# A linear-attention block and a gated GLU on one core: VectorE's work on the turned denominators, the weight forms and b's seeds is offered later, and small loads change queues

## The chip, the cores and the metric

The kernel runs on one core of one Trainium2 chip. A core has five engines with a queue of instructions each: TensorE (matrix products, into PSUM), VectorE, ScalarE, GpSimd and SyncE (SP). In the profile they are PE, DVE, ACT, POOL and SP. DMA transfers are issued from SP's and from GpSimd's queue here. Engines wait for each other by semaphores; an engine that waits holds everything behind in its own queue. The metric is the time of one execution in microseconds; lower is better.

## The reference

With S = 2048 tokens of width D = 640, 32 heads of width 20, and F = 1536, the output is `g * a + (1 - g) * b`, where `g` is one gate per token:

```python
g = _sigmoid((x * gate_w).sum(-1, keepdims=True))
phi = lambda t: jnp.where(t > 0, t + 1, jnp.exp(t)) + 1e-6
# a: linear attention
kv = jnp.einsum("bhsd,bhse->bhde", phi(k), v)
z = jnp.einsum("bhsd->bhd", phi(k))
num = jnp.einsum("bhqd,bhde->bhqe", phi(q), kv)
den = jnp.einsum("bhqd,bhd->bhq", phi(q), z)[..., None] + 1e-6
a = (num / den).transpose(...).reshape(B, S, D) @ wo
# b: gated linear unit
h = _sigmoid(x @ w_gate) * (x @ w_up)
b = h @ w_down
```

Each token and head has one denominator `den`, a sum over the 20 features of phi(q) weighted by `z`. All is float32.

## The kernel before

**Numbers and products.** Every float32 operand of a product is split into a high and a low part in TensorE's faster float32 format, and a product is three matmuls (`mm3`: high by high, high by low, low by high; lines 417 to 419). The high part is made by ScalarE (line 433), the low part by a subtraction on VectorE (line 437). On top of this, the products use Strassen- and Winograd-like schemes of seven products in place of eight, so there are many sums of operands on VectorE and of results in PSUM. A `Block` has seven such products, its steps `s1` to `s7`, of six or nine matmuls each.

**Stages.** Tokens come in four groups of 512 (g = 0 to 3). First the keys and the matrix phi(k)^T x are made (to about 140 us of the trace). Then, for the token groups 2 and 3 (`pr` = 1) and after that for 0 and 1 (`pr` = 0), the queries are made (`q_phase`), and then b's GLU in `f_phase`: twelve chunks f of 128 hidden columns, with steps (f, 1) to (f, 7). Odd chunks also carry the products with `w_down` of the pair before (`down_pair`, four parts d0 to d3). In the second `f_phase`, chunks 1 to 11 are `EBlock`s, which fold the fifth part of the inner dimension into fewer matmuls (line 428) with the help of weight forms ("e" forms): three small VectorE operations of 128 x 128 on pieces `d` and `u` of the weights that are loaded from DRAM (`queue_e`, line 1435 and on). Step s3 is the first that reads them. Last comes the attention product: phi(q), divided by the denominator and multiplied by the gate, is multiplied by the matrix M made of kv and wo (`ABlock`, `a_unit`). It accumulates in PSUM on a start value, "b's seed", which is b times the gate row 1 - g (`seed_b`).

**Denominators.** `queue_dens` is called in the second `f_phase`, in chunk 2 for groups 2 and 3 and in chunk 7 for groups 0 and 1. It sums phi(q), loaded as `pden` from DRAM, with weights `zcol` into `fac` (five operations a group), stores the sum (`den_dram`), loads it back turned, in four parts of 32 partitions (`turn_in`, `fac<-den_dram`), adds the four column blocks, takes the reciprocal, multiplies by the gate rows `gs` (`factor`, line 1609 and on), stores that (`fac_dram`) and loads it back four times over (`turn_out`, `fac<-fac_dram`). `pq_scale` multiplies phi(q) by `fac` later (line 441, `pl<-pl,fac` and `hf<-hf,fac`).

**The order of the work.** Nothing is ordered at run time: each engine runs its queue in program order. A planner in Python (`Order`) makes that order while the program is built. It keeps a clock for TensorE, ScalarE and VectorE with fixed costs (`v_cost(w)` is 0.07 us and w / 960), and between TensorE's steps, in `fill`, it puts the VectorE and ScalarE items in that it has been given. An item has a cost, a function, a key and a function `ready`: it is not placed before TensorE's or its own engine's clock has reached that time, and not when its engine would end more than a slack (0.6 us on ScalarE, 1.2 us on VectorE) behind TensorE. There are several lists: urgent items (`first`), streams with a due time, the plain list, then a lazy list, a `chain` (only its first item may be placed; the denominators are here) and a spare list (forms of M, through the single buffer `mt`). A stream's item is placed without regard to the slack 2 us ahead of its due time. `need(key)` places an item at once, where TensorE's next step needs it.

The planner believes times for DMAs too (`Rings`, `Ring`, from line 316): two rings, SP's with 0.38 us per issue and a lag of 1.5 us, GpSimd's with 0.55 us and 2.2 us, shared bandwidth, and 0.5 us at the end. `order.when(x)` is the time at which x is believed to have landed:

```python
took = 1.25 * max(1, n // r) * (7 + 0.0377 * r) / 16e3
self.cell = self.rings.issue(self.n, start + self.lag, took)
```

Here n is a transfer's bytes and r the bytes of a run. For some items a margin is added to that time already: `DEN_LAG = 5.0` (line 315) for the five sums of a denominator, for the stores out of `mt`, half of it for M's rows. If a transfer lands later than believed, the instruction that reads it stands on its engine and waits, with everything behind it.

**Loads at the end of the second `f_phase`.** After its last step the code issues, on SP, `load_p(3)`, `load_m(1)` (960 KB of M's forms into `ws`), `load_b(2)` (three loads of 256 KB, `bl<-b_dram`), the gate row of group 3, `load_b(3)` and `load_ms(0)`; the gate rows of groups 0 and 1 (`omg<-gate_dram`) are loaded later, after the first half of the attention blocks of groups 2 and 3.

Of the kernel before, what the change touches and what calls it, by code (L numbers as in the profile page):

```python
# [14 lines left out]
P = 128  # L15
S, D, F = 2048, 640, 1536
H, DH = 32, 20
KC = D // P
# [296 lines left out]
DEN_LAG = 5.0  # L315
# [65 lines left out]
def v_cost(w):  # L381
    return 0.07 + w / 960

@with_exitstack
def gated_mix_kernel(ctx: ExitStack, tc: tile.TileContext, x0, xt, xn, wk, wv, wo, wst_q, wst_f, out_t):
# [6 lines left out]
    order = Order()  # L392
    rings = Rings()
    sp, gp = Ring(nc.sync, order, rings, 0, 0.38, 1.5), Ring(nc.gpsimd, order, rings, 1, 0.55, 2.2)

    def f32(ap):
        return ap.bitcast(F32)
# [37 lines left out]
    def vec2(out, a, b, op, after=""):  # L435
        order.on_vec(width(out), after, 1.0, out, a, b)
        nc.vector.tensor_tensor(out, a, b, op=op)  # L437

    def vec3(out, a, scalar, b, op0, op1, after=""):
        order.on_vec(width(out), after, 1.0, out, a, b)  # L440
        nc.vector.scalar_tensor_tensor(out, a, scalar, b, op0=op0, op1=op1)

    def vec1(out, a, s0, s1=None, op0=OP.mult, op1=None, after=""):
        order.on_vec(width(out), after, 1.0, out, a)
        if op1 is None:
            nc.vector.tensor_scalar(out, a, s0, None, op0=op0)
        else:
            nc.vector.tensor_scalar(out, a, s0, s1, op0=op0, op1=op1)
# [10 lines left out]
    def add(out, a, b, after=""):  # L459
        vec2(out, a, b, OP.add, after)  # L460
# [11 lines left out]
    def fac_tile(dt=F32):  # L472
        return common.tile([P, NG, TG], dt, name="fac", tag="fac")

    fac = fac_tile()
# [6 lines left out]
    gate_rep = dram.tile([S // P, H, P], F32, name="gate_rep")  # L482
    den_dram = dram.tile([P, NG, TG], F32, name="den_dram")
    fac_dram = dram.tile([P, NG, P], F32, name="fac_dram")
# [588 lines left out]
    g = GTBatch(0, [0])  # L1073
# [8 lines left out]
    for c in range(1, 4):  # L1082
        ck = chunks[c]
        if c == 1:
# [14 lines left out]
            g = GTBatch(c, batches[c])  # L1099
# [59 lines left out]
        if c == 3:  # L1159
# [15 lines left out]
            W, WT = {}, {}  # L1175
# [22 lines left out]
        if c > 1:  # L1198
            g = GTBatch(c, batches[c])
# [53 lines left out]
    def tt(name, dt=F32, shape=(P, TG)):  # L1253
        return pw.tile(list(shape), dt, name=name, tag="t", bufs=4)

    def ct(name, dt=F32, shape=(P, TG)):
        return pw.tile(list(shape), dt, name=name, tag="c", bufs=5)
# [177 lines left out]
    def queue_e(f):  # L1435

        n = ("f", 0, f)
        d, u = EW[f, "d"], EW[f, "u"]
        dh, dl = d[:, :P], d[:, P:]
        uh, ul = (W[n, 1][c][:, 2 * P:] for c in range(2))  # L1440

        def fn():
            vec3(u[:, :P], f32(dh), -1 / UP, f32(ul), OP.mult, OP.add)
            vec3(u[:, P:], f32(ul), UP, f32(uh), OP.mult, OP.add)
            vec3(dl, f32(dh), 1 / UP, f32(dl), OP.mult, OP.add)
        order.add(0, 3 * v_cost(P), fn, ("e", f), lambda: max(order.when(d), order.when(WT[n, 1])),
                  stream=("e", f), due=order.due((0, f, 3)))

    def queue_et(late):
# [125 lines left out]
    def queue_dens(*gs2):  # L1575

        nonlocal fac
        if "f" in EF:
            EF.pop("f")
            fac = fac_tile()  # L1580
        st = {}

        def load(g, u):
            if u < KC:
                st[g, u] = tt("pden")
                gp.dma_start(st[g, u], p_dram[:, u, g])
                st["at", g, u] = lambda: order.when(st[g, u])

        def one(g, u):
            td = fac[:, g]  # L1590
            if u == 0:
                vec1(td, st[g, u], zcol[:, 0:1], zeps[:, 0:1], OP.mult, OP.add)
            else:
                vec3(td, st[g, u], zcol[:, u:u + 1], td, OP.mult, OP.add)
            load(g, u + 2)
            if u == KC - 1:
                gp.dma_start(den_dram[:, g], td)
                st["at", g, u + 1] = lambda: order.when(den_dram[:, g])

        def turn_in(g):  # L1600
            for j in range(4):
                js = slice(j * H, (j + 1) * H)
                gp.dma_start(fac[js, g].rearrange("h (d c) -> h d c", c=P),
                                  den_dram[:, g, j * P:(j + 1) * P].rearrange("(d h) c -> h d c", h=H))
            st[g, "gs"] = tt("gs")[:, :P]
            sp.dma_start(st[g, "gs"], gate_rep[4 * g:4 * g + 4].rearrange("i h c -> (i h) c"))
            st["at", g, KC + 1] = lambda: max(order.when(fac[:, g]), order.when(st[g, "gs"]))

        def factor(g):
            td = fac[:, g]  # L1610
            q = td[:, :P]
            add(td[:, :2 * P], td[:, :2 * P], td[:, 2 * P:])
            add(q, q, td[:, P:2 * P])
            order.on_vec(5 * P, "")
            nc.vector.reciprocal(q, q)
            vec2(q, q, st[g, "gs"], OP.mult)
            gp.dma_start(fac_dram[:, g], q)
            st["at", g, KC + 2] = lambda: order.when(fac_dram[:, g])

        def turn_out(g):  # L1620
            for d in range(4):
                sp.dma_start(fac[d * H:(d + 1) * H, g].rearrange("h (j c) -> h j c", c=P),
                                  fac_dram[:, g].rearrange("(j h) c -> h j c", h=H))
        order.add(0, 0, lambda: [load(g, u) for u in range(2) for g in gs2], chain=True)
        for u in range(KC):
            for g in gs2:
                order.add(0, v_cost(TG), lambda g=g, u=u: one(g, u), None, lambda g=g, u=u: st["at", g, u]() + DEN_LAG, chain=True)
        for n, (v, fn) in enumerate(((0, turn_in), (2.0, factor), (0, turn_out))):
            for g in gs2:
                order.add(0, v, lambda g=g, fn=fn: fn(g), ("fac", g) if n == 2 else None,  # L1630
                          lambda g=g, n=n: st["at", g, KC + n](), chain=True)

    sp.t = max(sp.t, gp.cell[0])
    load_w()
# [457 lines left out]
    OMG = {}  # L2092
# [17 lines left out]
    def load_omg(g):  # L2110

        OMG[g] = down_pool[1].tile([P, TG], F32, name="omg", tag="omg") if g == 2 else tt("omg")
        sp.dma_start(OMG[g], gate_dram[1, g * TG:(g + 1) * TG].partition_broadcast(P))
# [281 lines left out]
    def f_phase(pr, q, hooks={}):  # L2395
# [86 lines left out]
        for f in range(FC):  # L2482
# [3 lines left out]
            if f in dens[pr]:  # L2486
                queue_dens(*dens[pr][f])
# [88 lines left out]
    q = q_phase(1, lambda k: [(b12h[:, k], b12l[:, k])], extra)  # L2576
# [32 lines left out]
    q = q_phase(0, lambda k: [tuple(t[:, k] for t in b12)], {0: [lambda: next(down), more_c], 1: [lambda: next(down)], 8: [lambda: order.need((nx[1], 6), False), early_omg], 9: [lambda: queue_ds(LAST), lambda: queue_df(LAST)], 10: [lambda: queue_last("T2", "T3", "T4")]})  # L2609

    groups = (2, 3, 0, 1)
    PL, PQ, BL, MHL, PT, MS, X3, ST = {}, {}, {}, {}, {}, {}, [], []

    def x2_tile(name="pl", dt=F32):
        return px.tile([P, 2, TG], dt, name=name, tag="x2", bufs=10)
# [4 lines left out]
    def load_m(i):  # L2620

        while any(it[3] == "m" for it in order.spare) or order.pend:
            order.need("m")
            order._flush()
        n = (0, 7, 10)
        t = (wf_tile, ws_tile)[i]().rearrange("p a b -> p (a b)")[:, :(n[i + 1] - n[i]) * D]
        for j0, j1 in ((0, 4), (4, 7), (7, 10))[2 * i:2 + i]:
            sp.dma_start(f32(t[:, (j0 - n[i]) * D:(j1 - n[i]) * D]),
                         mp_dram.rearrange("p a b c -> p (a b c)")[:, j0 * D:j1 * D])
        for j in range(n[i], n[i + 1]):  # L2630
            MHL[divmod(j, 2)] = t[:, (j - n[i]) * D:(j - n[i] + 1) * D]
# [40 lines left out]
    def load_b(g):  # L2672

        if g < 2:
            BL[g] = {o: tb[:, o, g] for o in range(KC)}
        else:
            if g == 2:
                t = x2_tile("bl")
                BL[g] = {4: ct("bl"), 0: t[:, 0], 2: t[:, 1]}
            else:  # L2680
                t = down_pool[1].tile([P, D], F32, name="mr", tag="mr")
                BL[g] = {4: t[:, :TG]}
            for o, t in BL[g].items():
                sp.dma_start(t, b_dram[:, o, g - 2])
# [19 lines left out]
    def pq_tiles(g):  # L2704

        t = [x2_tile("pq", F32R) for _ in range({2: 4, 3: 2}.get(g, KC))]
        PQ[g] = [(x[:, 0], x[:, 1]) for x in t]
        if g == 2:
            X3.extend(x3_tile("pq") for _ in range(4))
            PQ[g].append((X3[2][:, 2], X3[3][:, 2]))  # L2710
        elif g == 3:
            PQ[g] += [(X3[0][:, u], X3[1][:, u]) for u in range(3)]
# [56 lines left out]
        vec2(ps, BL[g][o], OMG[g], OP.mult)  # L2769

    def b_at(g, o):
        return max(order.when(BL[g][o]), order.when(OMG[g]) if g in OMG else 1e9)

    def queue_seed(g, o, tag):
        order.add(0, v_cost(TG), lambda: seed_b(g, o, tag), ("b", g, o), lambda: b_at(g, o), first=True)
# [153 lines left out]
    pq_tiles(2)  # L2929
    queue_pq(2)  # L2930
    load_p(3)
    load_m(1)
    pq_tiles(3)
    queue_scale(3)
    queue_pq(3)
    load_b(2)
    load_omg(3)
    load_b(3)
    load_b(0)
# [105 lines left out]
```

## Time and profile before

| | |
|---|---|
| three runs | 730.4, 733.19, 735.96 us; median 733.19 |
| profiled execution | 734.18 us; the span from its first to its last instruction 732.5 us |
| TensorE clock granted in it | 0.998 of full |
| TensorE busy | 721.5 us, 98% of the span |
| VectorE busy | 589.2 us, 80% |
| ScalarE busy | 366.1 us, 50% |
| GpSimd busy (its DMA issues among it) | 118.0 us, 16% |
| DMA | 177.6 MB, 242 GB/s on the mean |

The second `f_phase` lies between about 445 and 640 us of the trace, the attention product between 659 and 729. In the profile's views a line such as `DVE fac L437 <- DMA fac<-den_dram: 6.4, 1, 6.4` says who waited (engine, the tile it writes, the line of the kernel), for whom, and how long in total, how often, and the longest. In a timeline the first number is the start in microseconds from the span's start, the second the duration; what stands in brackets is the engine's idle time just before and what ended it. `out<-in` are the kernel's own names of the tiles. Matmuls overlap, so the step from start to start is shorter than one matmul's duration. Most operations are recorded at the line of a helper (417 to 419, 428: matmuls; 433: ScalarE; 437, 441, 448: VectorE; 374: DMA issues).

### The profile page before, as it was taken

The page shows a single profiled execution, that of the slowest core. Times are in us where ns is not written, and L with a number is a line of the kernel's source. Part 1 is how long each engine was busy: PE and PEld are TensorE (multiplying, and loading weights), DVE is VectorE, ACT ScalarE, POOL GpSimd, SP SyncE. Part 2 cuts the span into 40 slices and gives each one's busy share as a digit, 9 for nine tenths or more (in the row PEclk, how much of TensorE's full clock was granted, in tenths as well). Part 3 has the DMA queues.
Part 4 walks back from the last instruction along what each step waited for, and adds up shares of the span by engine and source line. Part 5 has one row for each costly group of instructions (what it writes and reads, how often), then busy time and mean ns, then how long its engine had stood idle before and what let it go on. Part 6 is the DMA issues. An engine that isn't in the chain of part 4 may idle for free.

```text
span 732.5 us, 9922 instructions
## 1 busy us (share of the span) xinstructions
PE 721.5 (98%) x3401; PEld 607.3 (83%) x3401; DVE 589.2 (80%) x1045; ACT 366.1 (50%) x682; POOL 118.0 (16%) x199
## 2 busy tenths in 40 slices
PE   9999999999999999999999999998999999999898
PEld 8999999888888888888888888886788888887676
DVE  4988878987777889888998886665776888689886
ACT  5764749267557644444456762363332333335351
POOL 0311111113212211211121122013001131000200
PEclk9999999999999999999999999999999999999999
DMA  8474658698787856657688787889588897779623
GB/s 269 116 205 112 177 137 259 158 326 297 278 323 258 308 205 230 244 221 263 246 330 277 218 287 271 325 283 316 190 250 296 284 323 247 256 287 330 124 42 130
DMA packets 75657, 177.60 MB, mean 242 GB/s; under 512 B 12266, under 2 KB 34170, under 8 KB 73430
## 3 DMA queue, kind: packets, MB, share of 16 engines
q1 hardware_dynamic: 55654, 104.03, 43.5%
q0 software_dynamic: 19664, 72.70, 29.0%
q8 instruction: 27, 0.44, 0.2%
q10 hardware_dynamic: 288, 0.23, 0.1%
q14 instruction: 24, 0.20, 0.1%
HBM read 104.62 MB, written 67.33 MB: 235 GB/s over the span
## 4 chain that ended last, share of the span: by engine, by line
PE 92%; DVE 3%; DMA 2%; ACT 1%; issue 1%; POOL 0%; SPq 0%; DVEq 0%; POOLq 0%; ACTq 0%
PE ch L418 10%; PE ch L419 10%; PE ch L417 10%; PE cc L418 7%; PE cc L419 7%; PE cc L417 7%; PE dd L417 7%; PE dd L418 7%; PE dd L419 7%; PE rot L419 5%; PE rot L418 5%; PE rot L417 5%; PE ch L428 1%; PE cc L428 1%; DMA fac<-den_dram 1%; DMA omg<-gate_dram 1%
## 5 line engine op out<-in xcount | busy, mean ns | idle before, releaser
L437 DVE TENSOR_TENSOR hf<-c,hf 128x512 fp32r<-128x512 f32 x77 | 52.6, 687 | 26.0 <-ACT hf L433 25.5
L433 ACT ACTIVATE hf<-c 128x512 fp32r<-128x512 f32 (+1 forms) x79 | 48.8, 625 | 39.6 <-DVE c L437 39.6
L433 ACT ACTIVATE c<-ch 128x512 f32<-128x512 f32 x43 | 25.7, 597 | 77.8 <-PE ch L428 56.9
L417 PE MATMUL ch<-xth,ws 128*128 128x512 f32 x108 | 42.2, 391 | 0.0
L419 PE MATMUL ch<-xth,ws 128*128 128x512 f32 x108 | 42.1, 390 | 0.0
L418 PE MATMUL ch<-xtl,ws 128*128 128x512 f32 x108 | 42.1, 389 | 0.0
L437 DVE TENSOR_TENSOR tb<-rot,tb 128x512 f32<-128x512 f32 x60 | 39.0, 684 | 1.9 <-PE rot L419 1.9
L437 DVE TENSOR_TENSOR c<-cc,c 128x512 f32<-128x512 f32 x38 | 26.2, 688 | 17.0 <-ACT c L433 10.1
L437 DVE TENSOR_TENSOR c<-c,c 128x512 f32<-128x512 f32 x48 | 33.0, 688 | 2.6 <-ACT c L433 2.0
L437 DVE TENSOR_TENSOR tb<-dd,tb 128x512 f32<-128x512 f32 x41 | 28.1, 686 | 8.3 <-PE dd L419 8.3
L433 ACT ACTIVATE dd<-ch 128x512 f32<-128x512 f32 x22 | 12.8, 583 | 36.2 <-PE ch L428 20.4
L433 ACT ACTIVATE c<-dd 128x512 f32<-128x512 f32 x21 | 12.5, 597 | 35.6 <-PE dd L428 17.0
L417 PE MATMUL dd<-xrh,wg 128*128 128x512 f32 x73 | 28.7, 394 | 1.5 <-ACT dd L433 1.5
L437 DVE TENSOR_TENSOR wst<-wst 128x256 f32<-128x256 f32 (+2 forms) x69 | 27.4, 412 | 1.4
L418 PE MATMUL dd<-xrl,wg 128*128 128x512 f32 x73 | 28.4, 390 | 0.0
L419 PE MATMUL dd<-xrh,wg 128*128 128x512 f32 x73 | 28.4, 389 | 0.0
L417 PE MATMUL cc<-xbh,ws 128*128 128x512 f32 x71 | 27.6, 389 | 0.0
L418 PE MATMUL cc<-xbl,ws 128*128 128x512 f32 x71 | 27.6, 389 | 0.0
L419 PE MATMUL cc<-xbh,ws 128*128 128x512 f32 x71 | 27.6, 389 | 0.0
L433 ACT ACTIVATE c<-c 128x512 f32<-128x512 f32 x31 | 19.5, 628 | 10.5 <-DVE c L437 10.2
L433 ACT ACTIVATE cx<-ch 128x512 f32<-128x512 f32 x16 | 9.6, 597 | 29.1 <-PE ch L419 28.9
L419 PEld LDWEIGHTS ch<-xth,ws 128*128 128x128 f32 x108 | 20.3, 188 | 4.5 <-DVE ws L437 0.3
(755 smaller groups left out, 2403.2 us busy)
## 6 DMA issues: line engine op xcount, KB each, us to landing
wf<-ws POOLq DMA_DIRECT2D x12, 1152.0 KB, 7.7
wst<-wst_f SPq DMA_DIRECT2D x12, 640.0 KB, 4.9
wf<-wg POOLq DMA_DIRECT2D x12, 640.0 KB, 6.8
wd<-wd POOLq DMA_DIRECT2D x12, 640.0 KB, 8.1
wg<-wf SPq DMA_DIRECT2D x12, 640.0 KB, 6.2
wf<-wd SPq DMA_DIRECT2D x10, 640.0 KB, 7.8
ws<-wf SPq DMA_DIRECT2D x23, 256.0 KB, 4.8
xnst<-xn SPq DMA_DIRECT2D x16, 320.0 KB, 4.1
```

The source lines that it names most:

```text
L417: nc.tensor.matmul(out, l_hi, r_hi, start=first, stop=False, skip_group_check=True)
L418: nc.tensor.matmul(out, l_hi, r_lo, start=False, stop=False, skip_group_check=True)
L419: nc.tensor.matmul(out, l_lo, r_hi, start=False, stop=last, skip_group_check=True)
L428: nc.tensor.matmul(out, w, x, start=False, stop=n == len(singles) - 1, skip_group_check=True)
L433: nc.scalar.activation(out, src, fn, **kw)
L437: nc.vector.tensor_tensor(out, a, b, op=op)
```

## The change

Five things are edited; no computation is added or left out.

- The "e" weight forms become ready 5 us (`DEN_LAG`) after their pieces are believed to have landed.
- The gate rows `gs` are loaded from GpSimd's queue instead of SP's, and so are the four parts of `turn_out`.
- `factor` becomes two items of the chain: the two adds (`factor`), and the reciprocal, the multiplication by `gs` and the store (`turn_over`). Their stated costs are 0.6 and 0.9 in place of 2.0. The adds become ready 5 us after the parts of `turn_in` (and `gs`) are believed to have landed; `turn_over` is ready at any time, but as the chain goes in order, it comes after both groups' adds.
- b's seeds (and the scaling of b by the gate row) become ready 2.5 us after the gate row is believed to have landed, or with b, whichever is later.
- `load_m(1)` is issued after `load_b(2)` instead of before `pq_tiles(3)`.

```diff
-        order.add(0, 3 * v_cost(P), fn, ("e", f), lambda: max(order.when(d), order.when(WT[n, 1])),
+        order.add(0, 3 * v_cost(P), fn, ("e", f), lambda: max(order.when(d), order.when(WT[n, 1])) + DEN_LAG,
                   stream=("e", f), due=order.due((0, f, 3)))
...
             st[g, "gs"] = tt("gs")[:, :P]
-            sp.dma_start(st[g, "gs"], gate_rep[4 * g:4 * g + 4].rearrange("i h c -> (i h) c"))
+            gp.dma_start(st[g, "gs"], gate_rep[4 * g:4 * g + 4].rearrange("i h c -> (i h) c"))
             st["at", g, KC + 1] = lambda: max(order.when(fac[:, g]), order.when(st[g, "gs"]))
 
         def factor(g):
...
             add(td[:, :2 * P], td[:, :2 * P], td[:, 2 * P:])
             add(q, q, td[:, P:2 * P])
+
+        def turn_over(g):
+            q = fac[:, g, :P]
             order.on_vec(5 * P, "")
             nc.vector.reciprocal(q, q)
             vec2(q, q, st[g, "gs"], OP.mult)
             gp.dma_start(fac_dram[:, g], q)
-            st["at", g, KC + 2] = lambda: order.when(fac_dram[:, g])
+            st["at", g, KC + 3] = lambda: order.when(fac_dram[:, g])
 
         def turn_out(g):
             for d in range(4):
-                sp.dma_start(fac[d * H:(d + 1) * H, g].rearrange("h (j c) -> h j c", c=P),
+                gp.dma_start(fac[d * H:(d + 1) * H, g].rearrange("h (j c) -> h j c", c=P),
                                   fac_dram[:, g].rearrange("(j h) c -> h j c", h=H))
...
-        for n, (v, fn) in enumerate(((0, turn_in), (2.0, factor), (0, turn_out))):
+        for g in gs2:
+            st["at", g, KC + 2] = lambda: 0.0
+        for n, (v, fn) in enumerate(((0, turn_in), (0.6, factor), (0.9, turn_over), (0, turn_out))):
             for g in gs2:
-                order.add(0, v, lambda g=g, fn=fn: fn(g), ("fac", g) if n == 2 else None,
-                          lambda g=g, n=n: st["at", g, KC + n](), chain=True)
+                order.add(0, v, lambda g=g, fn=fn: fn(g), ("fac", g) if n == 3 else None,
+                          lambda g=g, n=n: st["at", g, KC + n]() + (DEN_LAG if n == 1 else 0.0), chain=True)
...
     def b_at(g, o):
-        return max(order.when(BL[g][o]), order.when(OMG[g]) if g in OMG else 1e9)
+        return max(order.when(BL[g][o]), order.when(OMG[g]) + DEN_LAG / 2 if g in OMG else 1e9)
...
     load_p(3)
-    load_m(1)
     pq_tiles(3)
     queue_scale(3)
     queue_pq(3)
     load_b(2)
+    load_m(1)
     load_omg(3)
```

## The prediction

> **What bounds the kernel now.** The page comes first: its span, its busy shares, its chain by engine.
>
> ```profile
> span 732.5 us, 9922 instructions
> ...
> PE 721.5 (98%) x3401; PEld 607.3 (83%) x3401; DVE 589.2 (80%) x1045; ACT 366.1 (50%) x682; POOL 118.0 (16%) x199
> ...
> PE 92%; DVE 3%; DMA 2%; ACT 1%; issue 1%; POOL 0%; SPq 0%; DVEq 0%; POOLq 0%; ACTq 0%
> ```
>
> TensorE is busy for 98% of the span, and the change removes no matmul. It can only win back time in which TensorE waits, so the next view is TensorE's own waits (total, times, longest). One start-up entry is left out:
>
> ```profile
> PE ch L418 <- DVE pq L437: 2.9, 1, 2.9
> PE dd L417 <- ACT dd L433: 1.7, 2, 1.5
> PE ch L417 <- ACT c L433: 1.4, 1, 1.4
> ...
> PE cc L418 <- DVE pt L437: 0.2, 1, 0.2
> PE dd L417 <- DVE dd L437: 0.2, 1, 0.2
> ```
>
> That is 6.4 us in six waits, all behind VectorE, or behind a ScalarE that follows it. What delayed those two stands in the chain of waits in order of time (start, us) and in the timelines of VectorE and TensorE (start, us, instruction, idle before it). Place one, in that order:
>
> ```profile
> 496.71 7.53 DMA fac<-den_dram
> ```
>
> ```profile
> 497.13 0.68 DVE L437 TENSOR_TENSOR hf<-c,hf 128x512 fp32r<-128x512 f32 x1
> 504.26 0.75 DVE L437 TENSOR_TENSOR fac<-fac 128x256 f32<-128x256 f32 x2 [6.45 <-DMA fac<-den_dram]
> ...
> 506.25 0.68 DVE L437 TENSOR_TENSOR c<-cc,c 128x512 f32<-128x512 f32 x1
> ```
>
> ```profile
> 499.50 0.61 PE L428 MATMUL cc<-xbh,ws 128*128 128x512 f32 x2
> ...
> 508.13 0.50 PE L417 MATMUL ch<-xth,wu 128*128 128x512 f32 x1 [1.45 <-ACT c L433]
> ...
> 511.71 0.50 PE L417 MATMUL dd<-xrh,wg 128*128 128x512 f32 x1 [1.47 <-ACT dd L433]
> ```
>
> VectorE stands 6.45 us in `factor`, for the turned denominators. The instruction queued behind it, `c<-cc,c`, could have run from 500.1, when its cc product was finished, and ran at 506.25. All that follows is as late, and TensorE waits at 508 and again at 511.7. Place two:
>
> ```profile
> 683.16 7.45 DMA omg<-gate_dram
> ```
>
> ```profile
> 688.01 0.69 DVE L437 TENSOR_TENSOR mt<-ch,mt 128x512 f32<-128x512 f32 x1 [0.50 <-PE ch L419]
> 690.71 1.30 DVE L437 TENSOR_TENSOR dd<-tb,omg 128x512 f32<-128x512 f32 x2 [2.01 <-DMA omg<-gate_dram]
> 691.92 0.69 DVE L437 TENSOR_TENSOR rot<-tb,omg 128x512 f32<-128x512 f32 x1
> ...
> 694.32 3.09 DVE L437 TENSOR_TENSOR pq<-hf,pq 128x512 fp32r<-128x512 f32 x5
> ```
>
> ```profile
> 691.59 0.39 PE L419 MATMUL ch<-pq,ws 128*128 128x512 f32 x1
> 691.82 0.39 PE L417 MATMUL ch<-pq,wf 128*128 128x512 f32 x1
> 695.06 0.50 PE L418 MATMUL ch<-pq,wf 128*128 128x512 f32 x1 [2.86 <-DVE pq L437]
> ...
> 696.20 0.63 PE L419 MATMUL ch<-pq,wf 128*128 128x512 f32 x1
> ...
> 699.19 0.48 PE L417 MATMUL dd<-pq,wf 128*128 128x512 f32 x1
> ```
>
> The three seeds of group 0 stand 2.01 us for the gate row and take 1.8 us more (690.71 to 692.5), all ahead of the `pq` that TensorE needs for its second matmul. After the wait TensorE runs slow: seven matmuls take 2.99 us (696.20 to 699.19), 0.43 each, where the step before the wait is 0.23 (691.59 to 691.82).
>
> **The change part by part.** *Factors offered 5 us later, in two items.* The planner puts `factor` on VectorE when it believes that the four parts have landed. By the kernel's own constants (Ring, Rings) that is 2.2 us of lag, 0.26 for 128 runs of 512 bytes and 0.5, so 3.0 us after an issue; the chain's row has 7.53. It is 4.5 us short, and the new 5 us cover that. VectorE, free from 497.81, then does `c<-cc,c` and what follows at their own time and meets the two adds at 502.8 or later, since the planner also wants VectorE's own work to be at most 0.6 us ahead; the data is there at 504.26. At most 1.5 us of waiting remain. I take none of it as TensorE's: the whole stall with the 2.0 us of factor work behind it (504.26 to 506.25) held `c<-cc,c` up by 6.1 us and cost TensorE some 3.5, so it absorbs more than 1.5. Gain: the `dd<-ACT dd` and `ch<-ACT c` waits, 1.7 + 1.4, and for each of the three 0.15 by which start to start exceeds the wait in place two (695.06 − 691.82 − 0.23 = 3.01 against 2.86): **3.6 us**. The reciprocal half follows the second group's adds in the chain; VectorE's work stays 2.0 us. Nobody needs the factors soon (instructions on the tile `fac`: ns least/median/most, first and last start):
>
> ```profile
> L374 POOL DMA_DIRECT2D fac<-den_dram x16: 549/549/576, 495.1 to 601.0; - x16
> L374 SPq DMA_DIRECT2D fac<-fac_dram x16: 325/382/634, 536.3 to 620.3; - x16
> ...
> L441 DVE SCALAR_TENSOR_TENSOR pl<-pl,fac x9: 681/685/687, 641.3 to 665.6; 128x512 f32<-128x512 f32 x9
> ```
>
> The last turned part is issued at 620.3 and the first factor is read at 641.3: 21 us of cover, against 5 us of lag and some 5 for the split. With the cover gone, each further microsecond would be TensorE's.
>
> *Gate rows and turning on GpSimd's queue.* Sixteen `fac<-fac_dram` parts (0.38 us, 6 us in all) and four gate rows leave SP, on whose queue no wait of TensorE's hangs: 0. On GpSimd's they cost 0.55 us each, by the `fac<-den_dram` row, 11 us in 130 on an engine busy 16%. New there: the parts wait on the queue for the factor's store to land, and behind them stand the `pden` loads (whose readers have 5 us of lag already) and the stores of `mt`, a single buffer that ScalarE writes next. The planner leaves 5 us after such a store: I take 0, and the last rival is this cover gone. `gs` is issued behind the four parts of its group and read only by the second item: 0.
>
> *Weight forms 5 us later.* Their lead over the matmul that reads them, in two odd chunks:
>
> ```profile
> 515.14 0.28 DVE L441 SCALAR_TENSOR_TENSOR ws<-ws,wu 128x128 fp32r<-128x128 f32 x1
> ...
> 622.73 0.28 DVE L441 SCALAR_TENSOR_TENSOR ws<-ws,wu 128x128 fp32r<-128x128 f32 x1
> ```
>
> ```profile
> 516.84 0.39 PE L428 MATMUL ch<-ws 128*128 128x512 f32 x1
> ...
> 626.24 0.39 PE L428 MATMUL ch<-ws 128*128 128x512 f32 x1
> ```
>
> The lead is 3.5 us, and 1.7 in the chunk behind the stall; neither matmul waits. Five microseconds use it up, so the forms are forced at the start of the step that needs them. Its six earlier matmuls give 6 x 0.23 = 1.4 us, the first form takes 0.3. Lower bound 0; upper bound, with VectorE 1.5 us ahead of TensorE there, 0.4 in each of five odd chunks, 2.0. I take **+0.2**, near the 1.7 us row, which is just this case.
>
> *b's seeds 2.5 us later.* The planner believes 1.5 + 0.84 + 0.5 = 2.9 us for a gate row on SP; the chain's row has 7.45. So 2.5 us do not cover the error. But they exceed one step (nine matmuls, 2.05 us), so the seeds go behind the two last scalings, two or three `pq` and an add: five or six instructions of 0.60 us (the two seeds from 690.71 to 691.92). VectorE, free at 688.70, reaches them at 691.7, after the landing at 690.6. The first `pq` ends at 688.70 + 2 x 0.60 + 0.69 = 690.6, before TensorE asks for it at 691.82 + 0.23. Gain 3.0 for the wait, and 2.99 − 7 x 0.23 = 1.4 for the slow steps: **4.4 us**. I tie the slow steps to this wait, since the step before it is 0.23. The Trainium skill ("TensorE: Matmul & The Clock Gate", Part 1) has the clock fall to half after an idle window of about 3.4 us, in windows that run freely; the wait here is shorter and the steps slowed all the same. Taken strictly, the rule would leave the 1.4 us in place, and the sum would be 1.4 us higher.
>
> What is late next is VectorE's `pt`, for which TensorE waits 0.2 us today. Ahead of it VectorE waited here:
>
> ```profile
> 698.02 1.29 DVE L437 TENSOR_TENSOR pq<-hf,pq 128x512 fp32r<-128x512 f32 x2 [0.61 <-ACT pq L433]
> 700.58 1.90 DVE L437 TENSOR_TENSOR pq<-hf,pq 128x512 fp32r<-128x512 f32 x3 [1.26 <-ACT pq L433]
> ```
>
> TensorE comes 4.4 us earlier. VectorE gains its 2.01 us and, as ScalarE's copies of TensorE's products come earlier too, these 0.61 and 1.26: 3.9. The rest, **+0.5 us**, stays as new waiting (bounds 0 and 4.4 − 2.0 = 2.4).
>
> *load_m(1) behind load_b(2)*, in SP's, VectorE's and TensorE's timelines:
>
> ```profile
> 646.93 0.35 SPq L374 DMA_DIRECT2D ws<-mp_dram  x1
> 647.33 2.68 SPq L374 DMA_DIRECT2D bl<-b_dram  x3
> ```
>
> ```profile
> 661.72 1.30 DVE L437 TENSOR_TENSOR dd<-bl,omg 128x512 f32<-128x512 f32 x2
> ```
>
> ```profile
> 663.73 0.39 PE L419 MATMUL dd<-pq,ws 128*128 128x512 f32 x1
> ```
>
> The b loads pass the larger one. The wait `dd<-DVE dd` (0.2, 0.3 with its start) can go: **−0.3**. The larger one gains three loads of 256 KB ahead of it. Those three, queued behind it, were in use at 661.72; if the queue lands in order, it had landed by then, and it is read 2.0 us later: on time, or a fraction late. Bounds 0 and +1; I take 0, as the loads that pass it are the smaller ones.
>
> **Sum.** 734.18 (the profiled execution: its span and 1.7 us around it) − 3.6 − 4.4 − 0.3 + 0.2 + 0.5 = **726.6**. The profiled execution is 1.0 us above the median of the three runs, 733.19, which spread over 5.6 us. Waits for DMA landings are what differs from run to run, and just these go, so I take off only 0.2: **726.4**.
>
> **The rivals.** *The seeds still meet the gate row early* (0.18): 2.5 us against an error of 4.6. For it are the numbers, against it the five instructions that come between. If the order stays, so does place two: 734.2 − 3.6 − 0.3 = 730.3; taken half, 728.5.
>
> *The odd chunks pay it back* (0.08): forced behind a longer VectorE queue, each of the five loses 1.5 us, what the forms' lead shrinks by beyond the 1.7 us case. 726.4 + 7.5 = 734, no change.
>
> *GpSimd's queue holds ScalarE* (0.10, slower). The view of the tile `fac_dram` has, for its stores and parts:
>
> ```profile
> DMA to landing us min/median/max: 1.8/5.1/6.0
> ```
>
> The planner believes 3.0, so the queue stands 2 to 3 us longer than planned before the parts, which then take 4 x 0.55 = 2.2. Together that is the 5 us of margin. If the parts are held, the next `mt` store is late and ScalarE stands at the single `mt`, with the copies out of PSUM behind it. It decides from about 1 us a part. With 3 us of TensorE's in each of four groups: 726.4 + 12 = 738.4. Against it: sixteen issues of the same shape took 576 ns at most, beside a VectorE at 80%. The Trainium skill ("SBUF — State Buffer", the section on SBUF's two separate sides) warns of just this: VectorE operations that use both ports keep GpSimd from writing descriptors, so it advises another queue; the 549 to 576 ns show nothing of it here.
>
> **Numbers.** Forecast 0.64, own range 724.5 to 728.5. With the first rival: 724.3 to 731.8; outside lie the other two and a little below. One per cent, 7.3 us, is about what a measurement of this kernel tells from no change. Faster by that is under 725.9, inside the forecast's own range, with half of it below: 0.32. Slower by that (740.5) is the bad half of the last rival and what I have not seen: 0.07. The rest, 0.61, is within 1%.
>
> **What would show it.** Step one: no VectorE wait on `fac<-den_dram` above 1.5 us and no TensorE wait behind it. Step two: `dd<-tb,omg` behind the first `pq`, no `ch<-DVE pq` wait, no 0.43 us steps. The added terms: waits of `ch` on `ws` forms in odd chunks, of `ch` or `cc` on `pt`. The slower rival: ScalarE at `mt` behind its store. I am wrong if TensorE's waits after the start still add up to over 4 us.

## The result, and the profile after

The changed kernel takes 725.24 us (median of 10 executions, 724.46 to 729.69), the kernel before 732.73 in the same comparison (median of 10, 730.4 to 735.96). The ratio is 0.9896, with a 95% interval of 0.9873 to 0.9919: 1.0% less time. The prediction was 726.4 us, with 724.3 to 731.8 as its range. The profiled execution took 725.48 us. Its page begins:

```profile
span 723.7 us, 9909 instructions
...
PE 718.2 (99%) x3401; PEld 605.9 (84%) x3401; DVE 588.5 (81%) x1045; ACT 366.0 (51%) x682; POOL 129.4 (18%) x219
...
PE 97%; DMA 1%; DVE 1%; ACT 0%; issue 0%
```

The last line is the chain of waits by engine: TensorE carries 97% of it, 92% before. GpSimd is busy for 11 us more, as worked out. TensorE's waits, behind the start-up entry:

```profile
PE ch L417 <- ACT pt L433: 0.5, 1, 0.5
PE ch L417 <- DMA ws<-wf: 0.4, 1, 0.4
PE ch L418 <- DVE pt L437: 0.2, 1, 0.2
```

Six waits of 6.4 us have become three of 1.1 us. Place one in VectorE's timeline:

```profile
499.66 0.69 DVE L437 TENSOR_TENSOR c<-cc,c 128x512 f32<-128x512 f32 x1 [2.33 <-PE cc L428]
...
509.38 1.40 DVE L437 TENSOR_TENSOR fac<-fac 128x256 f32<-128x256 f32 x4
...
511.30 0.94 DVE L1618 RECIPROCAL fac<-fac 128x128 f32<-128x128 f32 x1
...
513.09 0.94 DVE L1618 RECIPROCAL fac<-fac 128x128 f32<-128x128 f32 x1
```

`c<-cc,c` runs at 499.66, when its product is there, and not at 506.25. The adds of both groups run at 509.38 without a wait, the reciprocals behind them. Place two in the same view:

```profile
683.13 0.69 DVE L437 TENSOR_TENSOR mt<-ch,mt 128x512 f32<-128x512 f32 x1 [0.17 <-PE ch L419]
...
684.93 1.29 DVE L437 TENSOR_TENSOR pq<-hf,pq 128x512 fp32r<-128x512 f32 x2
686.14 0.68 DVE L437 TENSOR_TENSOR st<-cc,st 128x512 f32<-128x512 f32 x1
686.74 0.68 DVE L437 TENSOR_TENSOR pq<-hf,pq 128x512 fp32r<-128x512 f32 x1
687.34 0.69 DVE L437 TENSOR_TENSOR dd<-tb,omg 128x512 f32<-128x512 f32 x1
688.28 1.29 DVE L437 TENSOR_TENSOR pq<-hf,pq 128x512 fp32r<-128x512 f32 x2 [0.25 <-ACT pq L433]
```

Three `pq` and an add now stand ahead of the first seed, which does not wait.

Where the 8.7 us between the two profiled executions are shows in TensorE's timeline, at matmuls that both kernels have in the same place of the order. Before (499.50, the first of them, stands in the prediction):

```profile
526.20 0.39 PE L428 MATMUL ch<-xbl,ws 128*128 128x512 f32 x1
...
645.36 0.62 PE L428 MATMUL cc<-xbh,ws 128*128 128x512 f32 x2
...
728.56 0.28 PE L419 MATMUL rot<-pq,ws 128*128 128x256 f32 x1
```

After:

```profile
499.00 0.62 PE L428 MATMUL cc<-xbh,ws 128*128 128x512 f32 x2
...
521.70 0.39 PE L428 MATMUL ch<-xbl,ws 128*128 128x512 f32 x1
...
641.50 0.62 PE L428 MATMUL cc<-xbh,ws 128*128 128x512 f32 x2
...
719.98 0.28 PE L419 MATMUL rot<-pq,ws 128*128 128x256 f32 x1
```

| stretch | before, us | after, us | gain, us |
|---|---|---|---|
| up to the first | 499.50 | 499.00 | 0.5 |
| place one | 26.70 | 22.70 | 4.0 |
| the rest of the second f_phase | 119.16 | 119.80 | −0.6 |
| the attention product, with place two | 83.20 | 78.48 | 4.7 |

The first line is a difference between two executions, not the change: TensorE's matmul at 100 us, long before the first instruction that the change moves (444 us, the weight forms), is 0.47 us earlier already. What was given back lies in these rows of after's timeline:

```profile
548.34 0.50 PE L417 MATMUL ch<-xth,ws 128*128 128x512 f32 x1 [0.39 <-DMA ws<-wf]
...
697.83 0.50 PE L417 MATMUL ch<-pt,ws 128*128 128x512 f32 x1 [0.53 <-ACT pt L433]
698.56 0.50 PE L418 MATMUL ch<-pt,ws 128*128 128x512 f32 x1 [0.23 <-DVE pt L437]
```

The second and third are the `pt` waits of the prediction. The first, a weight load of chunk 7 that landed late, was in none of its steps.

### The profile page after: what moved, and what is told of

Read it like the earlier page. It is cut to its first block, busy times and chain, and to the rows that moved or that the text cites. A ratio compares the mean times of both kernels' runs of the same rounds, so it can differ in the third digit from the quotient of the medians.

```text
span 723.7 us, 9909 instructions
## 1 busy us (share of the span) xinstructions
PE 718.2 (99%) x3401; PEld 605.9 (84%) x3401; DVE 588.5 (81%) x1045; ACT 366.0 (51%) x682; POOL 129.4 (18%) x219
## 4 chain that ended last, share of the span: by engine, by line
PE 97%; DMA 1%; DVE 1%; ACT 0%; issue 0%
PE ch L418 11%; PE ch L417 11%; PE ch L419 10%; PE cc L417 8%; PE cc L418 8%; PE cc L419 8%; PE dd L417 7%; PE dd L418 7%; PE dd L419 7%; PE rot L418 5%; PE rot L419 5%; PE rot L417 5%; PE ch L428 2%; PE cc L428 1%; DMA ws<-wf 1%; PE rot L1708 1%
## 5 line engine op out<-in xcount | busy, mean ns | idle before, releaser
L417 PEld LDWEIGHTS ch<-xth,ws 128*128 128x128 f32 x108 | 20.3, 188 | 4.8 <-DMA ws<-wf 0.8
L419 PEld LDWEIGHTS ch<-xth,ws 128*128 128x128 f32 x108 | 20.3, 188 | 4.5 <-DVE ws L437 0.3
```

What stands on the lines that cost most here:

```text
L417: nc.tensor.matmul(out, l_hi, r_hi, start=first, stop=False, skip_group_check=True)
L419: nc.tensor.matmul(out, l_lo, r_hi, start=False, stop=last, skip_group_check=True)
```

## The experiments

My theory was the prediction's: two places, two waits for DMAs that the planner believed too early, and the other edits worth nothing. Unless another number is named, differences are between medians, each experiment against the kernel before on the same chip, whose medians lay between 732.10 and 732.85 us.

### Each place alone, and both

The factors alone: `turn_over` split off, the adds 5 us later, all else as before.

```diff
-        for n, (v, fn) in enumerate(((0, turn_in), (2.0, factor), (0, turn_out))):
+        for n, (v, fn) in enumerate(((0, turn_in), (0.6, factor), (0.9, turn_over), (0, turn_out))):
...
+                          lambda g=g, n=n: st["at", g, KC + n]() + (DEN_LAG if n == 1 else 0.0), chain=True)
```

> Of the change, this has the factors alone: two items, the adds 5 us later; the queues, the weight forms, the seeds and load_m(1) are as before. Theory: place one goes and place two stays. VectorE's 6.45 us on fac<-den_dram falls to at most 1.5 us, TensorE's two waits of 1.4 to 1.5 us at 508 and 511 go, and the kernel is 3.6 to 4.2 us faster than before (about 729). TensorE still waits about 2.9 us for pq near 691. Rival: the moved work meets something else on VectorE, and what is gained at 510 is paid back by the end of the second f_phase; then it is within 1 us of before.

Measured: 729.61 us, ratio 0.9967 (0.9950 to 0.9983), 2.9 us less. Place one is gone (its stretch takes 22.69 us, as in the changed kernel), place two is there, in VectorE's and then TensorE's timeline:

```profile
685.78 1.30 DVE L437 TENSOR_TENSOR dd<-tb,omg 128x512 f32<-128x512 f32 x2 [1.64 <-DMA omg<-gate_dram]
```

```profile
690.13 0.80 PE L418 MATMUL ch<-pq,wf 128*128 128x512 f32 x1 [2.49 <-DVE pq L437]
```

The gain is 0.7 us short of the lower end of what I expected: part of it is the late weights of chunk 7, which this kernel has too (0.2 us as a wait, 0.37 from start to start).

The seeds alone:

```diff
-        return max(order.when(BL[g][o]), order.when(OMG[g]) if g in OMG else 1e9)
+        return max(order.when(BL[g][o]), order.when(OMG[g]) + DEN_LAG / 2 if g in OMG else 1e9)
```

> Of the change, this has b's seeds 2.5 us later and nothing else. Theory: place two goes and place one stays. The wait of 2.9 us for pq near 691 and the slow matmuls of 0.43 us behind it go, some 0.5 us comes back as waits for pt, and the kernel is 3.9 to 4.9 us faster than before. Rival one, the clock's fall is not tied to this wait: the seven or eight steps of 0.43 us stay, and the gain is 2.5 to 3.5 us. Rival two, the seeds still meet the gate row early: VectorE still waits over 1 us on omg<-gate_dram, and the gain is under 2 us.

Measured: 727.77 us, ratio 0.9940 (0.9925 to 0.9955), 4.7 us less. TensorE's longest waits:

```profile
PE dd L417 <- ACT dd L433: 1.7, 2, 1.5
PE rot L528 <- PEq L3036: 0.8, 1, 0.8
PE ch L417 <- ACT c L433: 0.8, 1, 0.8
```

The one of VectorE's that is left in place one:

```profile
DVE fac L437 <- DMA fac<-den_dram: 5.8, 1, 5.8
```

No wait for `pq` and none for `omg`, no matmul step of 0.43 us behind the start, and a granted clock of 0.999 or 1.000 in all four executions: rival one (the clock falls anyway) and rival two (the seeds still meet the row) are both out.

Both together, with nothing else of the change:

> The factors (two items, 5 us later) and the seeds (2.5 us later) together; the weight forms, the queues and load_m(1) as before. Theory: the two places are the whole change and add up: 2.9 us measured for the factors alone and 4.7 for the seeds alone give 7.6 us below before, 724.9 us with before at 732.5, no more than 0.7 us from the changed kernel's 725.2. Rival: the other three edits carry part of it; then this is 1 to 3 us slower than the changed kernel.

Measured: 724.75 us, ratio 0.9897 (0.9874 to 0.9919), 7.4 us less, where the two alone add up to 2.9 + 4.7 = 7.6 and the whole change gave 7.5. Within the interval, some 1.6 us either way, the two places are all of it, and they add up.

### The lag or the split

The split without the 5 us (`+ 0.0` in place of `DEN_LAG`):

> The factors in two items as in the change, but without the 5 us: the adds are offered when the parts are believed to have landed. Theory: the planner's belief is the cause, not the size of the item. The adds stay at their old place in VectorE's order, VectorE waits there 5.5 to 6.5 us for fac<-den_dram, but only 0.75 + 0.6 us of work stands behind the wait in place of 2.0 us, so the kernel is at most 0.7 us faster than before. Rival: the long item of 2.0 us was what hurt, and splitting it gives most of the gain, 2.5 to 4 us.

Measured: 731.03 us, ratio 0.9971 (0.9952 to 0.9991), 1.4 us less, twice what I allowed and well under the rival's 2.5 to 4. VectorE's waits:

```profile
DVE fac L437 <- DMA fac<-den_dram: 8.9, 2, 6.9
```

It stands just as long for the parts. In place one 1.2 us of reciprocal and multiplication (0.94 and 0.29) no longer stand between the landing and `c<-cc,c`; the stretch takes 25.32 us in place of 26.70, and 0.8 of these 1.4 us come back as late weights of chunk 7. What the median holds beyond that isn't settled: six of its ten executions have a granted clock of 1.000, against 13 of 39 of the kernel before, and at 0.998 the medians, its four executions' and the 26 of before with 0.998 or less, are only 0.6 us apart (732.19 and 732.8).

The 5 us without the split:

```diff
-                          lambda g=g, n=n: st["at", g, KC + n](), chain=True)
+                          lambda g=g, n=n: st["at", g, KC + n]() + (DEN_LAG if n == 1 else 0.0), chain=True)
```

> The opposite half: the factor stays one item of 2.0 us, and is offered 5 us later. Theory: the 5 us do the whole of it. VectorE's wait on fac<-den_dram is under 1.5 us, TensorE's waits at 508 and 511 go, and the kernel is 3.3 to 4.2 us faster than before, as with both. Rival: an item of 2.0 us still holds c<-cc,c long enough that TensorE waits; then 1 to 2 us of the gain are missing.

Measured: 726.54 us, ratio 0.9927 (0.9910 to 0.9943), 5.9 us less, more than any theory said. No wait for `fac<-den_dram` is left, and the stretch of place one takes 22.69 us (22.70 with the split too), so the 5 us do the whole of place one. The rest came at place two, which this edit does not name. TensorE's timeline there:

```profile
684.67 0.50 PE L417 MATMUL ch<-hf,wf 128*128 128x512 f32 x1 [0.55 <-DVE mt L437]
...
688.21 0.50 PE L417 MATMUL ch<-pq,wf 128*128 128x512 f32 x1 [1.20 <-ACT pq L433]
688.94 0.50 PE L418 MATMUL ch<-pq,wf 128*128 128x512 f32 x1 [0.23 <-DVE pq L437]
```

The seeds still met the gate row (a VectorE wait of 1.7 us), but in a slightly other order, and TensorE waited three times, 2.0 us in all, instead of 2.86 at once; none was followed by slow matmuls. So the planner's order shifts far from an edit, and the time of a variant holds that too.

One item with its 5 us, and the seeds 2.5 us later:

> The factor as one item, 5 us later, and the seeds 2.5 us later; nothing else of the change. Theory: the split earns nothing and costs the late weights of chunk 7: with both groups' factors done at 509, four loads of M's rows and the next loads of phi(q) move ahead of them, and TensorE waits 0.6 us at 547. In one item the second group comes some 15 us later and this wait is absent. Place one then gives the full 4.0 us and place two 4.7: 723.8 us with before at 732.5, about 1 us below the changed kernel. Rival: the split is needed when the rest is in place, and this is 0 to 2 us slower than the changed kernel.

Measured: 723.49 us (723.03 to 724.13, four executions), ratio 0.9881 (0.9863 to 0.9900). With two edited lines it gains as much as the whole change: its interval overlaps that of the changed kernel. Against the two places with the split on the same chip (724.75, 724.06 to 725.35) it is 1.3 us lower. The reason that I gave was wrong: the wait for chunk 7's weights did not go.

```profile
PE rot L528 <- PEq L3036: 0.8, 1, 0.8
PE cc L417 <- DMA ws<-wf: 0.5, 1, 0.5
```

It has moved by a step (0.62 us from start to start). What is missing against the changed kernel are the waits for `pt`.

The changed kernel with the factor in one item again:

> The changed kernel with the factor in one item again (its 5 us kept, and the four other edits). Theory: as above, the wait of 0.6 us at 547 goes and nothing else comes: 0.3 to 0.9 us below the changed kernel, about 724.6 us. Rival: the item of 2.0 us holds up what TensorE waits for; 0.5 to 2 us above the changed kernel, with a new wait of TensorE near VectorE's reciprocal.

Measured: 724.35 us, ratio 0.9893 (0.9875 to 0.9910). No new wait near the reciprocals, and none for chunk 7's weights. The split is not needed. Whether it costs anything the intervals don't tell; in the traces, seven of the nine kernels with the split have TensorE late at that place (0.2 to 1.7 us from start to start), and one of the five without it.

### The other three edits, undone one by one

Weight forms ready without the 5 us (`+ DEN_LAG` taken out in `queue_e`):

> The changed kernel with the weight forms ready as before (no 5 us). Theory: the later forms cost and gain next to nothing; in the changed kernel their lead shrank to 0.55 us in chunks 3 and 11, and no matmul waited for them. Within 0.7 us of the changed kernel's 725.2. Rival one: the later forms are needed, as a form placed early would hold VectorE for its pieces; then 1 to 3 us slower, with VectorE waits for ws<-wf. Rival two: they cost what the prediction allowed, 0.4 us in each odd chunk; then 1 to 2 us faster.

Gate rows and `turn_out` on SP's queue again (`gp.dma_start` back to `sp.dma_start`, twice):

> The changed kernel with the gate rows gs and the turned parts on SP's queue again. Theory: the queue is worth nothing to TensorE as the kernel stands: within 0.7 us of the changed kernel. ScalarE's wait of 2.3 us at mt behind the store at 631.9 goes, as GpSimd's queue has no parts any more. Rival one: SP's issues hold up the weight loads of the second f_phase, 1 to 3 us slower with TensorE waits on ws<-wf. Rival two: GpSimd's queue costs TensorE time, and this is 1 us faster.

`load_m(1)` ahead of the `pq_tiles(3)` again:

> The changed kernel with load_m(1) at its old place, ahead of b's loads. Theory: 0 to 0.5 us slower than the changed kernel: the wait of dd for ws or dd near 661 (0.2 to 0.3 us) comes back, nothing else. Rival: the order matters more, because b's seeds of groups 2 and 3 then wait for bl; over 1 us slower with a VectorE wait on bl<-b_dram.

Measured: 724.46 us (ratio 0.9878, 0.9858 to 0.9898), 724.89 (0.9883, 0.9861 to 0.9905) and 723.71 (0.9867, 0.9846 to 0.9888). None is slower than the changed kernel, and all intervals overlap its own. So none of the three edits shows a gain here; what is well under the intervals' 1.5 us could hide.

- The forms: undone, VectorE waits 2.9 us again for pieces (2.5 for `ws<-wf`, 0.4 for `wu<-wf`), and no matmul waits with it. So the later forms took away VectorE waits that cost nothing.
- The queue: undone, ScalarE's wait at `mt` goes, as expected. The profiled execution has the late weights of chunk 7 at their longest, which is rival one's sign without its price; I have not traced what lengthens it there:

```profile
PE ch L417 <- DMA ws<-wf: 1.5, 1, 1.5
```

- `load_m(1)`: undone, the wait near 661 did not come back, and the two longer waits for `pt` went. ScalarE's timeline of the changed kernel and then of this one shows how:

```profile
689.86 0.60 ACT L433 ACTIVATE st<-ch 128x512 f32<-128x512 f32 x1 [0.59 <-PE ch L419]
690.35 2.71 ACT L433 ACTIVATE pq<-hf 128x512 fp32r<-128x512 f32 x5
```

```profile
689.10 1.15 ACT L433 ACTIVATE pq<-hf 128x512 fp32r<-128x512 f32 x2
690.14 0.60 ACT L433 ACTIVATE st<-ch 128x512 f32<-128x512 f32 x1
690.62 1.68 ACT L433 ACTIVATE pq<-hf 128x512 fp32r<-128x512 f32 x3
```

In the changed kernel the copy `st<-ch`, whose product is not there yet, stands ahead of five `pq` copies; ScalarE waits 0.59 us, and the `pq`, VectorE's differences and at last `pt` are later by as much as TensorE then waits. In the other order it fills its time with two `pq` first. But the two kernels above keep `load_m(1)` in its new place and have the good order too, and of the runs with the later seeds only the changed kernel and its variant with 32 issues (below) have the bad one. So it is not this edit alone, but the edits' combination, that happens to give the planner the bad order.

### GpSimd's queue pressed

Each turned part cut in four, then in two, so 64 and 32 issues in place of 16:

```diff
-                gp.dma_start(fac[d * H:(d + 1) * H, g].rearrange("h (j c) -> h j c", c=P),
-                                  fac_dram[:, g].rearrange("(j h) c -> h j c", h=H))
+                for j in range(4):
+                    gp.dma_start(fac[d * H:(d + 1) * H, g, j * P:(j + 1) * P], fac_dram[j * H:(j + 1) * H, g])
```

> The changed kernel with each part that is loaded back turned cut in four: 64 issues on GpSimd's queue in place of 16, in each of four groups 16 x 0.55 = 8.8 us in place of 2.2, more than the 5 us that the planner leaves behind a store of mt. It presses on the slower rival of the prediction. Theory: TensorE still has slack there, as no matmul waits for mt: within 1 us of the changed kernel. Rival (GpSimd's queue holds ScalarE through the single mt): a store of mt stands behind the parts, ScalarE waits at mt for several microseconds, and the time is 3 to 12 us above the changed kernel.

Measured: 734.94 us, ratio 1.0036 (1.0026 to 1.0047), 9.7 us above the changed kernel's median (10.3 when each is taken against the kernel before on its own chip). The rival's mechanism exists, with a longer chain than I had put down. The chain of waits, in order of time (start, us, what):

```profile
631.35 5.96 POOL fac L374 x13
...
641.94 8.76 DMA mp_dram<-mt
650.80 0.42 ACT mt L433
651.25 0.42 DVE mt L437
651.67 0.60 DVE c L437
652.28 0.61 DVE hf L437
```

The parts of the last two groups fill GpSimd's queue from 620.5 to 639.2. A store of `mt`, whose data VectorE had finished at 620.88, stands between them and is issued at 630.61, so ScalarE's next form comes at 633.75, where the changed kernel has it at 627.48. The store of that form is no longer held by the parts: VectorE writes its half of `mt` only at 640.82 to 641.64, the store goes out at 641.94 and lands at 650.70, 8.8 us later (3.2 us in the changed kernel, 631.86 to 635.06). Why the planner puts VectorE's half 6.3 us behind ScalarE's, and 2.5 us in the changed kernel, the runs don't show. ScalarE has stood 16.3 us at the single `mt` with the copies for TensorE behind it, and TensorE waits 7.5 us and runs slow after that. Nearly all of the loss is in this one place; the parts of the first two groups, near 520, cost nothing.

> The changed kernel with each turned part in two loads: 32 issues, 4.4 us a group. That is the point of about 1 us a part from which the prediction let the slower rival decide. Theory after the run with 64 issues (10 us slower, as the planner's own count of the queue put a store of mt behind the parts at 638.7, and its landing at 650.7 held ScalarE, then TensorE): the price is not proportional; as long as the last store of mt lands before ScalarE's next form is due, TensorE sees nothing. Within 1 us of the changed kernel, ScalarE's wait at mt 2 to 6 us. Rival: proportional to the issues, 3 us slower.

Measured: 725.38 us, ratio 0.9892 (0.9872 to 0.9912), the changed kernel's time. ScalarE's waits at `mt` in it:

```profile
ACT mt L433 <- DMA mp_dram<-mt: 4.1, 2, 3.4
ACT mt L433 <- DMA ms_dram<-mt: 3.5, 1, 3.5
```

and in the changed kernel:

```profile
ACT mt L433 <- DMA mp_dram<-mt: 2.8, 2, 2.3
```

The kernel before has no such wait. ScalarE takes up 7.6 us of them without one matmul being late behind them; 16 us in one piece are too much.

## Why the prediction was right

Both main steps held, and the runs of each alone and of both show it. The time came out 1.2 us below the sum, and this is the base of the sum, not its terms: they add up to 7.6 us of gain, and 7.5 were measured. That they agree so closely is partly luck, as terms that were missed cancel: 0.6 us of late weights and some 0.5 more for `pt` on one side; 0.4 more in place one, 0.2 more in place two and 0.4 of a wait near 675 that the prediction's list doesn't show (`cc<-pq`, 0.12 idle, 0.40 from start to start with the step behind it) on the other.

- **Place one**, 3.6 us: right in its mechanism, measured 4.0 in the stretch; 0.6 came back at 547, in a wait on another load (below). The 0.4 beyond the sum is in small delays of TensorE around the three waits, each under 0.15 us, which the sum left out. The old wait itself varies: in the trace of the seeds alone, with the same order there, the stretch takes 26.09 us in place of 26.70, so the gain is 3.4 to 4.0. That the long lag was what mattered, and not the split, was in the working (4.5 us of wrong belief against 5 us) and is shown by the two halves.
- **Place two**, 4.4 us: measured 4.7 with the seeds alone, with all that follows in it. In the trace of before the wait, the two steps behind it and the seven slow ones cost 4.6 us beyond 0.23 a step, and none of it is left after. The order came as worked out: the first seed at 687.34, where 691.7 less the 4.9 us won by then (`mt<-ch,mt` from 688.01 to 683.13) gives 686.8. The slow steps go with the wait. The rule of the Trainium skill ("TensorE: Matmul & The Clock Gate", Part 1), read strictly, with an idle window of about 3.4 us, would have left them; the measurement decides: the trace of the seeds alone has no such step.
- **`pt`**, +0.5 with bounds 0 and 2.4: the right place. In the changed kernel it is 1.4 us from start to start (0.69, 0.50 and 0.20), in the kernels with the later seeds and ScalarE's other order less than 0.5. What failed here is the size: I took ScalarE's copies to come earlier with TensorE's products and did not look at which copy the planner puts first.
- **`load_m(1)`**, −0.3: the wait went, but not by this edit. The wait of `dd` at 662 is gone with the load in its old place too, so it was not the load that removed it. This edit shows no gain.
- **The weight forms**, +0.2: the lead fell to 0.55 us in two chunks and no matmul waited. Not told apart from 0.
- **SP's and GpSimd's queues**, 0: right for GpSimd's. "On whose queue no wait of TensorE's hangs" was wrong for SP's: the weights of chunk 7 are on it. In the changed kernel four loads of M's rows are issued from 537.43 to 539.56, between two groups of these weights, and before the change they were issued at 532.16 to 533.44, ahead of them. The `ws` piece that TensorE waits for is issued behind them at 539.66, and the wait ends at 548.34, 8.7 us later; before, the piece for the same step was issued at 541.96 and landed at 546.65, 4.7 us later. The second group's adds moved from 538 to 509, and the spare work behind the chain moved with them. That these loads slow the piece is likely and not shown.
- **From the profiled execution to the median**, −0.2 for the waits that vary: too little. The profiled execution, 734.18, is 1.45 us above the median of ten, 732.73, and that is the error of the sum. Its granted clock isn't the reason: it is 0.998, and it lies 1.4 us above the median of the executions with 0.998 too (732.8, below). The trace of the seeds alone, where VectorE's and ScalarE's orders are the same up to 661 us, is 0.7 us earlier by 499 us and 0.6 shorter in place one, so next to that one, both the start and the old wait were long in the execution that the sum starts from.

The slower rival was rightly kept and rightly small. Its mechanism is there, though the store that ScalarE waits longest for is the one after the store that the parts hold; its margin is between 32 and 64 issues and not at the 1 us a part that I gave, and its price was put down as four times 3 us where the pressed kernel lost some 10 in one place.

## What to carry to other kernels

Where a planner orders the work, compare its believed landing with the trace's for each load that a busy engine waits on: one constant per load (5 us and 2.5 us here) gave all of the gain that can be told from none; with them in place, splitting items, moving queues and moving loads added nothing. A wait of a few microseconds on VectorE costs TensorE only what stands queued behind it and is due soon; 2.9 us of them, for the forms' pieces, were free, and 6.45 us cost 4.0 in another place. Small shifts reorder the plan more than 100 us further on, which is worth about 1 us either way here, so an edit worth less than that isn't measured by one variant.

## What the runs showed of the hardware

- The slow matmuls behind place two are a granted clock of one half, in a stretch of fixed length. Three stretches of the kernel before, around it (us, busy times of PE, PEld, DVE, ACT and POOL, granted clock, share of the DMA engines, GB/s):

```profile
692.56:695.97 3.41, 0.91 (x4) 0.77 (x5) 3.41 (x7) 1.61 (x4) 1.71 (x2) 1.00 0.19 17
695.97:699.38 3.41, 3.41 (x10) 2.66 (x9) 2.74 (x5) 1.63 (x3) 0.00 (x0) 0.50 0.89 144
699.38:709.00 9.62, 9.39 (x42) 7.28 (x41) 7.68 (x13) 5.42 (x11) 0.00 (x0) 1.00 0.06 24
```

- The half clock begins 0.9 us after TensorE is back at work (695.06). With the factors alone it lies at 689.97 to 693.39 and begins just before TensorE is back (690.13), with the split alone at 692.95 to 696.37, and in the run with 64 issues it begins at 649.06, within the wait of 7.5 us, and lasts 6.83 us, twice 3.41. So it isn't tied to the wait's end, but comes in stretches of 3.41 us. The Trainium skill ("TensorE: Matmul & The Clock Gate", Part 1) has its window run freely, and that agrees. Its 3.4 us of idleness don't: in the 3.41 us ahead of the half clock TensorE stood 2.50 us (before), 2.33 (the factors alone) and 2.22 (the split alone), from waits of 2.86, 2.49 and 2.79 us, while waits of 1.45 and 1.47 us at place one and three waits of 0.55, 1.20 and 0.23 us within 5 us were not followed by slow steps.
- The wait at place two, which the program has every time, seems to be followed by slow matmuls in some executions only. Of the 39 executions of the kernel before in the experiments, 13 had a mean granted TensorE clock of 1.000 and a median of 731.45 us, 26 had 0.998 or less and 732.8: 1.3 us apart, about what seven steps of 0.43 us in place of 0.23 cost. One stretch of 3.41 us at half clock makes a mean of 0.998. The profiled executions with that wait, all at 0.998, show those steps; none at 1.000 was profiled. That the wait is then cut in two by the border of two such stretches is a guess. By this reading the 1.4 us of the prediction are there in two of three executions, and the median has them. The slowest of the changed kernel's ten executions, 729.69 us, has 0.998 too; it was not profiled.
- The issue of a load says little on its landing: `omg` took 7.45 us in the kernel before, 7.1 with the factors alone (issued 678.55, landed 685.68) and 5.6 in the run with the 5 us and one item (677.02 to 682.63), on the same queue and at the same place of the program; with one item and the later seeds it took 4.45 (675.70 to 680.15). A margin made for one order has to hold for the next.
